# Handing out attention pieces in every second step of the first layer's loop, in groups of about four

## The chip, the cores and the metric

The kernel runs on one core of one Trainium2 chip. Times are device microseconds of one execution. The kernel before took 1786.16 us, the median of 3 runs (1785.07 to 1788.48).

## The reference

Attention over pooled keys and values, and two feed-forward layers behind it, all in float32:

```python
# q, k, v: (8 batches, 8 heads, 576 tokens, 64)
k_p = k.reshape(B, H, 72, 8, D).mean(axis=3)      # v_p in the same way
scores = softmax(q @ k_p.T / 8)                   # (576 x 72) for each batch and head
attn = scores @ v_p
x = attn.transpose(0, 2, 1, 3).reshape(4608, 512)
h = x @ w_in;  x1 = (h - tanh(h)) @ w_out         # 512 -> 2048 -> 512
h = x1 @ w2_in;  out = (h * cos(h)) @ w2_out      # the same sizes
```

## The kernel before, in words

**The layers.** The 4608 tokens go through each layer in 9 blocks of 512 (`i` from 0 to 8). A block has 16 steps (`f`), one for each 128 of the 2048 inner columns. A step of the first layer has 12 matmuls of 128x512 for `h` (`emit_h`, line 553), the elementwise work of `h - tanh(h)` on ScalarE and VectorE (`g1_act`, `g1_rest`, lines 564 to 576), the split of its result into a high and a low part (`g_second`, lines 582 and 583), and 12 matmuls that add an earlier step's part to the four accumulators (`emit_out1`, line 590). Numbers are carried as pairs of high and low parts, hence three matmuls for one product. `h` has two PSUM banks, the accumulators four.

**The attention.** It makes the `x` of the first layer, two blocks ahead of its use, in a ring of 1536 tokens (`xh`, `xl`). It is cut into pieces, and a list `items` holds them in a fixed order (lines 417 to 514). Batches are cut into tiles of up to 128 queries. A tile has `s1` (four transposes of q, line 332, evacuated by ScalarE at 334), `s2` twice (four score matmuls each, line 346; VectorE takes the maxima and subtracts them, lines 349 and 353, then ScalarE takes the exponential), `norm` on VectorE and GpSimd (lines 360 to 364), `s3` in two parts (four transposes at 375, two at 385; evacuated at 382 and 383, and at 391 to 393), and two or three tiles together have four `pv` (up to four matmuls, line 406; evacuated at 409 and 413). `kprep` (line 302) sets up the keys of a batch. All of these write to the two banks of `ps_a` through `att_tile`, in turn: a piece can't start before the piece two before it has been evacuated. Each piece has loads (`look` asks for those of the pieces up to `LOOK` = 4 ahead) and work that follows it (`post`: pooling of keys and values on GpSimd, `norm`, `place_v`). Some pieces are marked `apart`: they need what the piece just before them makes.

**Who gives them out.** At the head of each step of the first layer `slot` pops pieces (line 908). `index_for` says how many must be done by the end of block `i` (36, 55, 19, 30, 35, 35, 35 and 15 in blocks 0 to 7; five of the 55 only load). `slot` spreads them evenly: by the end of step `f` the share (f+1)/16 is due. It stops ahead of a piece that is `apart`, unless it is the first of the slot or the step is the last of the block.

**What sets the order.** Block 0 also converts the first layer's weights (`w1_tick`), blocks 1 to 7 those of the second layer (`w2_conv`). Until block 8 a planner puts each engine's instructions in order: where an engine is free by its modelled times, it takes the first instruction in program order that is ready by them. So an instruction whose inputs or whose buffer aren't ready lets later ones pass. On the chip each engine's order is then fixed. DMAs are issued from SP.

Of the kernel before, what the change touches and what calls it, by code (L numbers as in the profile page):

```python
# [38 lines left out]
def fused_kernel(ctx: ExitStack, tc: tile.TileContext, q, k, v, w1i, w1o, w2i, w2o, out):  # L39
# [8 lines left out]
    NF = DFF // 128  # L48
# [368 lines left out]
    items = []  # L417
# [98 lines left out]
    pos = [0]  # L516
# [14 lines left out]
    def pop():  # L531
        run_later()
        look(pos[0] + 1 + LOOK)
        it = items[pos[0]]
        pos[0] += 1
        fn = it["work"]()
        if fn:
            later.append(fn)
        later.extend(it["post"])
# [158 lines left out]
    block = [-1, 0, 0]  # L698

    def slot(want, i, f):  # L700
        if block[0] != i:
            block[:] = [i, want - pos[0], 0]
        due = -(-block[1] * (f + 1) // NF)
        first = True
        while block[2] < due and (first or f == NF - 1 or not items[pos[0]]["apart"]):
            pop()
            block[2] += 1
            first = False
# [84 lines left out]
    if True:  # L793
# [91 lines left out]
        for i in range(NB):  # L885
# [8 lines left out]
            for f in range(NF):  # L894
# [11 lines left out]
                else:  # L906
                    wi, wo = ring_i.pop(f), ring_o.pop(f)
                slot(want, i, f)
                do_second()
                run_later()  # L910
# [80 lines left out]
```

## Time and profile before

| | |
|---|---|
| median of 3 runs | 1786.16 us (1785.07 to 1788.48) |
| the profiled execution | 1787.28 us, span 1785.5 us |
| TensorE busy | 1737.2 us, 97% of the span |
| VectorE, ScalarE, GpSimd busy | 70%, 65%, 16% |
| mean granted TensorE clock | 0.989 of full speed |
| first layer, first matmul of block 0 to the end of block 8 | 59.20 to 992.24 us of the span |

The span splits in three: 59 us of attention before the first dense matmul, the nine blocks of the first layer with attention beside them, and nine blocks of the second layer, each of 16 like steps. Shares of busy time of TensorE are those of pipelined matmuls with modelled ends, so the distance between two starts says more than a duration.

### The profile page before, as it was taken

What the parts mean: (1) busy time and instruction counts of PE and PEld (TensorE: products, weight loads), DVE (VectorE), ACT (ScalarE), POOL (GpSimd) and SP (SyncE); (2) the same over time, 40 slices, a digit from 0 to 9 for tenths busy, and PEclk for the clock granted to TensorE, in tenths of its full rate; (3) what the DMA queues carried; (4) which work ended last, traced back from release to release, by engine and by line L of the source; (5) the groups of instructions that cost most, each with busy time, mean ns of one, the idle gap of its engine ahead of it and who ended that gap; (6) DMA issues with size and microseconds to landing.
All of it is one profiled execution on the core that took longest, in us unless ns stands there. A gap on an engine that the chain in (4) does not pass through costs nothing.

```text
span 1785.5 us, 22632 instructions
## 1 busy us (share of the span) xinstructions
PE 1737.2 (97%) x7960; PEld 1426.6 (80%) x7960; DVE 1244.2 (70%) x2109; ACT 1158.1 (65%) x2079; POOL 279.2 (16%) x342
## 2 busy tenths in 40 slices
PE   5989999999999999999999999999999999999999
PEld 3666878888888888888888888888888888888887
DVE  8699778778888887776666566565656666566655
ACT  4576767767677776766665666666666666666665
POOL 3764244213424141100000000000000000000000
PEclk8799999999999999999999999999999999999999
DMA  7565655645655554523277401010101010101000
GB/s 234 162 215 192 211 161 182 212 159 185 205 177 184 188 197 142 175 100 109 83 262 254 154 0 48 1 48 1 48 1 47 1 47 1 48 1 48 1 24 24
DMA packets 116402, 202.29 MB, mean 113 GB/s; under 512 B 45376, under 2 KB 61760, under 8 KB 116288
## 3 DMA queue, kind: packets, MB, share of 16 engines
q1 hardware_dynamic: 116288, 200.84, 33.9%
q8 instruction: 63, 1.03, 0.2%
q14 instruction: 51, 0.42, 0.1%
HBM read 156.76 MB, written 44.04 MB: 112 GB/s over the span
## 4 chain that ended last, share of the span: by engine, by line
PE 86%; DVE 5%; DMA 3%; ACT 2%; POOL 2%; issue 1%; SPq 0%; POOLq 0%; DVEq 0%; ACTq 0%
PE h L751 22%; PE acc L779 21%; PE h L553 19%; PE acc L590 18%; PE att L406 2%; PE att L346 2%; DMA kv<-in_k_dram 1%; POOL kv L269 1%; PE att L375 1%; DVE cva L168 1%; DMA raw<-in_moe_w_in_dram 1%; DVE gl L583 1%; DVE w L576 1%; PE att L332 1%; DVE w L575 1%
## 5 line engine op out<-in xcount | busy, mean ns | idle before, releaser
L751 PE MATMUL h<-xh,wi 128*128 128x512 f32 x1008 | 330.8, 389 | 0.0
L779 PE MATMUL acc<-wo,gh 128*128 128x512 f32 x1008 | 310.3, 389 | 0.0
L762 DVE SCALAR_TENSOR_TENSOR r<-kk,h 128x512 f32<-128x512 f32 (+1 forms) x145 | 99.1, 684 | 182.2 <-ACT kk L760 181.8
L751 PEld LDWEIGHTS h<-xh,wi 128*128 128x128 f32 x1008 | 189.3, 188 | 39.4
L779 PEld LDWEIGHTS acc<-wo,gh 128*128 128x128 f32 x1008 | 189.2, 188 | 39.3
L770 ACT ACTIVATE r<-r 128x512 f32<-128x512 f32 (+1 forms) x145 | 91.3, 630 | 195.2 <-DVE r L764 195.2
L553 PE MATMUL h<-xh,wi 128*128 128x512 f32 x576 | 199.8, 407 | 1.2 <-POOL wi L162 0.6
L553 PE MATMUL h<-xh,ri 128*128 128x512 f32 x576 | 196.2, 400 | 0.0
L571 DVE SCALAR_TENSOR_TENSOR w<-u,h 128x512 f32<-128x512 f32 x144 | 98.2, 682 | 140.6 <-ACT th L565 140.5
L751 PE MATMUL h<-xl,wi 128*128 128x512 f32 x504 | 196.1, 389 | 0.0
L779 PE MATMUL acc<-wo,gl 128*128 128x512 f32 x504 | 196.1, 389 | 0.0
L772 DVE TENSOR_TENSOR co<-co,h 128x512 f32<-128x512 f32 (+1 forms) x145 | 99.1, 684 | 117.6 <-ACT co L771 117.6
L590 PE MATMUL acc<-gh,wo 128*128 128x512 f32 x576 | 178.9, 392 | 0.0
L590 PE MATMUL acc<-gh,ro 128*128 128x512 f32 x576 | 177.4, 389 | 0.0
L759 ACT ACTIVATE kk<-h,bias_r 128x512 f32<-128x512 f32 (+1 forms) x145 | 99.6, 687 | 91.6 <-PE h L751 91.6
L564 ACT ACTIVATE u<-h 128x512 f32<-128x512 f32 x144 | 85.6, 594 | 91.6 <-PE h L553 91.1
L582 ACT ACTIVATE gh<-w 128x512 fp32r<-128x512 f32 x144 | 90.9, 631 | 66.3 <-DVE w L576 65.2
L583 DVE TENSOR_TENSOR gl<-w,gh 128x512 fp32r<-128x512 f32 x144 | 109.7, 762 | 28.2 <-ACT gh L582 26.0
L553 PEld LDWEIGHTS h<-xh,wi 128*128 128x128 f32 x576 | 109.7, 191 | 24.4 <-POOL wi L162 1.1
L590 PEld LDWEIGHTS acc<-gh,wo 128*128 128x128 f32 x576 | 109.1, 190 | 22.9
L576 DVE COPY_PREDICATED w<-u,th 128x512 f32<-128x512 uint32 x144 | 113.3, 787 | 19.1 <-ACT u L574 6.1
L590 PEld LDWEIGHTS acc<-gh,ro 128*128 128x128 f32 x576 | 108.1, 188 | 22.5
(165 smaller groups left out, 3530.4 us busy)
## 6 DMA issues: line engine op xcount, KB each, us to landing
ri<-s1i SPq DMA_DIRECT2D x64, 512.0 KB, 3.5
ro<-s1o SPq DMA_DIRECT2D x64, 512.0 KB, 3.4
raw<-in_moe_w_in_dram SPq DMA_DIRECT2D x32, 512.0 KB, 3.9
raw<-in_moe_w_out_dram SPq DMA_DIRECT2D x32, 512.0 KB, 4.0
x1s<-xe SPq DMA_DIRECT2D x36, 256.0 KB, 4.7
xr<-x1s SPq DMA_DIRECT2D x36, 256.0 KB, 3.9
out_dram<-xe SPq DMA_DIRECT2D x36, 256.0 KB, 2.1
kv<-in_k_dram SPq DMA_DIRECT2D x32, 256.0 KB, 3.9
```

The source lines that it names most:

```text
L553: nc.tensor.matmul(out=h[:, off:off + m], lhsT=wi[:, c, wsel, :], rhs=xt[:, r:r + m], start=(n == 0), stop=(n == 3 * KC - 1))
L571: nc.vector.scalar_tensor_tensor(w, u, C2, h, op0=ALU.mult, op1=ALU.mult)
L576: step_end[0] = nc.vector.copy_predicated(w, u.bitcast(U32), th)
L582: nc.scalar.activation(out=gh[:, a:e], in_=w[:, a:e], func=AF.Copy)
L583: nc.vector.tensor_tensor(gl[:, a:e], w[:, a:e], gh[:, a:e].bitcast(F32), op=ALU.subtract)
L590: nc.tensor.matmul(out=acc[d], lhsT=wo[:, wsel, d * 128:(d + 1) * 128], rhs=gt, start=(f == 0 and n == 0), stop=(f == NF - 1 and n == 2))
L751: nc.tensor.matmul(out=h, lhsT=wi[:, c, wsel, :], rhs=xt[:, o:o + BLK], start=(n == 0), stop=(n == 3 * KC - 1))
L759: nc.scalar.activation(out=kk[:, a:e], in_=h[:, a:e], func=AF.Identity, bias=bias_r, scale=INV_2PI)
L762: nc.vector.scalar_tensor_tensor(r[:, a:e], kk[:, a:e], -PI2_HI, h[:, a:e], op0=ALU.mult, op1=ALU.add)
L770: nc.scalar.activation(out=r[:, a:e], in_=r[:, a:e], func=AF.Abs)
L772: nc.vector.tensor_tensor(co[:, a:e], co[:, a:e], h[:, a:e], op=ALU.mult)
L779: nc.tensor.matmul(out=acc[t], lhsT=gt[:, t * 128:(t + 1) * 128], rhs=wo[:, wsel, :], start=(f == 0 and n == 0), stop=(f == NF - 1 and n = ...
```

## The change

In blocks 1 to 7 the odd steps get no pieces, and an even step gets what is due up to the end of the odd step behind it; a piece that is `apart` no longer ends the slot. In block 0 an even step gets the share of both steps too, an `apart` piece still ends the slot, an odd step gets what was left over, and the last two steps take all.

```diff
     def slot(want, i, f):
         if block[0] != i:
             block[:] = [i, want - pos[0], 0]
-        due = -(-block[1] * (f + 1) // NF)
+        due = -(-block[1] * (f + 2 - f % 2) // NF) if f % 2 == 0 or i == 0 else block[2]
         first = True
-        while block[2] < due and (first or f == NF - 1 or not items[pos[0]]["apart"]):
+        while block[2] < due and (first or f >= NF - 2 or i > 0 or not items[pos[0]]["apart"]):
             pop()
             block[2] += 1
             first = False
```

By the code, the pieces that do work in the 16 steps of a block are, before and after:

```
block 0: 3 2 2 2 3 2 2 2 3 1 3 2 3 2 2 2    5 0 4 0 5 0 4 0 4 1 4 0 3 2 4 0
block 1: 1 2 2 4 4 3 4 3 2 5 3 4 3 4 2 4    7 0 2 0 7 0 7 0 7 0 7 0 7 0 6 0
block 2: 2 1 1 1 1 2 1 1 1 1 2 1 1 1 1 1    3 0 2 0 3 0 2 0 2 0 3 0 2 0 2 0
block 3: 2 2 2 2 2 2 2 1 2 2 2 2 2 1 3 1    4 0 4 0 4 0 3 0 4 0 4 0 4 0 3 0
block 4: 3 2 2 2 2 3 2 1 3 2 3 2 2 2 2 2    5 0 4 0 5 0 4 0 4 0 5 0 4 0 4 0
blocks 5 and 6: as block 4
block 7: 1 1 1 1 1 1 1 1 1 1 1 1 1 1 1 0    2 0 2 0 2 0 2 0 2 0 2 0 2 0 1 0
```

## Rows read from the trace of the kernel before

**Rows 1.** The page's chain that ended last, by engine.
```profile
PE 86%; DVE 5%; DMA 3%; ACT 2%; POOL 2%; issue 1%; SPq 0%; POOLq 0%; DVEq 0%; ACTq 0%
```

**Rows 2.** Windows: length, busy time (instructions) by engine, granted clock; blocks 0, 1, 2, 3-6, 7, 8.
```profile
59.20:184.50 125.30, 112.77 (x494) 86.14 (x493) 109.14 (x167) 87.33 (x175) 71.00 (x79) 0.95 0.64 211
184.50:303.34 118.84, 114.26 (x573) 93.78 (x572) 92.06 (x179) 82.80 (x176) 45.94 (x65) 0.99 0.55 176
303.34:399.49 96.15, 96.15 (x457) 79.89 (x456) 71.20 (x123) 66.01 (x119) 21.86 (x25) 1.00 0.55 181
399.49:811.32 411.83, 409.93 (x2025) 341.23 (x2024) 331.73 (x593) 293.58 (x578) 108.64 (x131) 1.00 0.52 172
811.32:905.20 93.88, 93.88 (x437) 77.73 (x436) 62.26 (x105) 58.00 (x102) 2.29 (x2) 1.00 0.33 112
905.20:992.24 87.04, 87.04 (x385) 72.07 (x384) 55.65 (x85) 52.74 (x89) 0.00 (x0) 1.00 0.71 260
```

**Rows 3.** Waits of TensorE in block 0: total us, times, longest.
```profile
PE att L375 <- DVE eb L353: 5.7, 2, 3.8
PE att L406 <- DVE xl L413: 2.3, 1, 2.3
```

**Rows 4.** Waits of TensorE in block 1, the largest group.
```profile
PE att L375 <- DVE eb L353: 3.8, 2, 3.5
```

**Rows 5.** Waits of TensorE in blocks 2 to 7, all groups.
```profile
PE att L346 <- DVE ar L393: 0.9, 1, 0.9
PE att L346 <- ACT qT L334: 0.6, 1, 0.6
PE att L375 <- POOL kv L269: 0.4, 1, 0.4
```

**Rows 6.** Timeline of TensorE (start, length, what): lone pieces in block 2.
```profile
314.88 0.60 PE L375 MATMUL att<-ident,eb 128*128 128x128 f32 x4
315.23 0.48 PE L553 MATMUL h<-xh,wi 128*128 128x512 f32 x1
315.55 0.40 PE L553 MATMUL h<-xl,wi 128*128 128x512 f32 x1
...
320.81 0.38 PE L385 MATMUL att<-ident,eb 128*32 128x128 f32 x2
320.94 0.48 PE L553 MATMUL h<-xh,ri 128*128 128x512 f32 x1
```

**Rows 7.** Timeline of TensorE: the same two pieces in one slot, block 1.
```profile
196.52 0.60 PE L375 MATMUL att<-ident,eb 128*128 128x128 f32 x4
...
197.10 0.48 PE L553 MATMUL h<-xh,wi 128*128 128x512 f32 x1
```

**Rows 8.** Timeline of TensorE: a third piece of a slot, block 5.
```profile
604.01 0.66 PE L346 MATMUL att<-bd,qT 128*96 128x144 f32 x4
604.41 0.49 PE L553 MATMUL h<-xh,wi 128*128 128x512 f32 x1
604.75 0.73 PE L346 MATMUL att<-bd,qT 128*96 128x144 f32 x4
605.23 0.49 PE L553 MATMUL h<-xl,wi 128*128 128x512 f32 x1
605.55 0.62 PE L553 MATMUL h<-xh,wi 128*128 128x512 f32 x2
```

**Rows 9.** Timeline of TensorE: a third value piece, block 1.
```profile
295.62 0.40 PE L553 MATMUL h<-xh,ri 128*128 128x512 f32 x1
296.52 0.39 PE L406 MATMUL att<-ah,vbd 128*128 128x320 f32 x1 [0.51 <-DVE xl L413]
```

**Rows 10.** Timeline of VectorE: two score pieces evacuated, block 4.
```profile
502.27 0.80 DVE L349 TENSOR_REDUCE mx<-att 96x4 f32<-96x288 f32 x2
503.00 0.80 DVE L353 TENSOR_TENSOR eb<-att,mx 96x288 f32<-96x288 f32 x2
```

**Rows 11.** Window around the long wait of block 1 (columns as in rows 2).
```profile
226.60:238.80 12.20, 8.69 (x41) 7.01 (x40) 10.23 (x19) 9.10 (x18) 5.00 (x6) 0.86 0.49 164
```

## The prediction, made before the changed kernel was run

> **What bounds the kernel now.** I read the page first: the chain that ended last is 86% TensorE, 5% VectorE, 3% DMA [rows 1]. The change touches only the attention pieces, and those run beside blocks 0 to 7 of the first layer, so the second view is a table of windows over that layer (a window runs from the first matmul of a block's first step to that of the next block; blocks 3 to 6 stand together) [rows 2]. Block 8 holds no attention: 87.04 us for 16 steps, so a step of 12 + 12 dense matmuls costs 5.44 us, 0.227 us a matmul. What a block has above 87.04 us is what its attention costs. Counting the code's list, blocks 0 to 7 get 36, 50, 19, 30, 35, 35, 35 and 15 pieces that do work (block 1 gets five more that only load):
>
> - blocks 2 to 7: 9.11 us in block 2, 411.83 - 4 x 87.04 = 63.67 us in blocks 3 to 6, 6.84 us in block 7: 79.6 us over 169 pieces, 0.471 us a piece. The reader should see that it doesn't hang on density: 0.48 in block 2 and 0.46 in block 7 at about one piece a step, 0.47 in blocks 3 to 6 at two.
> - block 1: 31.80 us over 50 pieces at three or more a step, 0.64.
> - block 0: 38.26 us over 36 pieces, 1.06. Weights are converted here too: VectorE is busy 109.1 of 125.3 us, and TensorE's clock was granted at 0.95 of full, against 1.00 from block 2 on.
>
> The third view, who waited for whom on TensorE, says how much of this is waiting: 8.0 us in the two largest groups of block 0 [rows 3], 3.8 us in the largest of block 1 [rows 4], and only 1.9 us in all of blocks 2 to 7 [rows 5]. So in blocks 2 to 7 the attention is nearly at the cost of its own matmuls: there is little left that another grouping could win there, and much that it could lose.
>
> **The change part by part.** No work is added or removed: the same 260 pieces run in the same order, each with its matmuls, evacuations and loads. What moves is when they are handed out.
>
> *Fewer borders between attention and dense matmuls.* One could hope that four pieces together save borders. A lone piece of four transposes takes 0.35 us to the first dense matmul, and that one 0.32 to the next instead of 0.227, so 0.09 for the border; a lone piece of two transposes takes 0.13 us to the dense matmul, 0.22 with such a border [rows 6]. The same two pieces in one slot take 0.58 us [rows 7]: with one border 0.67 us, against 0.35 + 0.09 + 0.22 = 0.66 apart. The border saved comes back in that it is only the last transpose before dense work that the next matmul overlaps. I take 0; the bounds are 0 and a gain of 0.09 us for each of some 40 borders less in blocks 2 to 7, 3.6 us.
>
> *Pieces that find both spare PSUM banks taken.* All pieces of these blocks write to two buffers (`ps_a`), so from the third piece of a slot on each needs the evacuation of the piece two before it. From the code: third and later pieces of a slot number 5, 19, 0, 1, 4, 4, 4, 0 in blocks 0 to 7 now, and 17, 34, 3, 14, 19, 19, 19, 0 after: 61 more in blocks 2 to 7, 15 more in block 1, 12 more in block 0. What such a piece does now can be seen. The planner doesn't let TensorE stand: it slips the piece in between the dense matmuls of the same step, where it reckons the bank to be free. In [rows 8] the third piece of a slot comes behind one dense matmul: that one takes 0.34 us to the piece instead of 0.227 (+0.11), the piece takes 0.48 us to the next dense matmul, and that one 0.32 (+0.09): 0.68 us. The like piece ahead of it takes 0.40 us, 0.49 with a border. So a piece that is slipped in costs 0.19 us more than one at a border, without a wait worth the name. A less lucky one is the third of four value pieces in [rows 9]: TensorE stood at it for VectorE's evacuation, 0.90 us instead of 0.23, +0.67. VectorE shows why: the two score pieces of one slot are evacuated together, 0.80 + 0.80 us one behind the other, and the first bank is given back only by the second of those pairs [rows 10]. With four or five pieces in a slot that queue is twice as long, while what the planner reckoned with is not what the chip does. What is queued behind a waiting piece is everything on TensorE, since its matmuls run in order.
>
> Bounds for one more third-or-later piece: 0 (the planner finds a place where the bank has been free for long) and 0.67 us. The value in between I take from density. Block 1 is the one block that already runs at the new density (three to four a step). Without its one long wait of 3.5 us [rows 4] and the slow clock around it (granted 0.86 over 12.2 us, so about 1.7 us lost) [rows 11] its pieces cost (31.80 - 5.2) / 50 = 0.53 us, 0.06 us above the 0.471 of blocks 2 to 7. For the 135 pieces of blocks 3 to 6 that is 8.2 us, or 0.135 us for each of the 61 third-or-later pieces: between 0 and the 0.19 of [rows 8], as when some get through free. Block 1 itself: 15 x 0.135 = 2.0 us; its first slot now also holds one tile's whole chain (transposes, scores, softmax, transposes, values), which stood in four steps. I put that into the same price.
>
> *Empty odd steps.* They run at 5.44 us and let ScalarE and VectorE catch up; in blocks 3 to 6 VectorE is busy 331.7 of 411.8 us [rows 2], so nothing was owed there. Worth 0.
>
> *Block 0.* Pieces come up to half a step earlier, five and four together, against a VectorE that has 13% left. The waits there could shrink or grow; the bounds are -4 us (half of the 8.0 us) and +4. I take 0.
>
> *Loads.* Each pop asks for the loads of four pieces ahead. With four in two steps instead of two in each the lead is the same two steps; in block 1, with seven in a slot, it is shorter for the last three. Loads are issued where their buffers come free, so I take 0 and leave up to 2 us in the range.
>
> Sum: 8.2 + 2.0 = +10.2 us. The profiled execution took 1787.28 us (span 1785.5), 1.1 above the median of 1786.16: 1797.5 on its own scale, **1796.4 us** against the median.
>
> The Trainium skill, Perfetto Trace Analysis, section Optimization Strategy, holds that the same gap repeating on the engine that ought to be saturated can mean too little PSUM for the next tile to be allocated. By that rule every third and fourth piece would show a gap as in [rows 9]. The trace so far agrees only in part: [rows 9] shows such a gap, [rows 8] none, and the sum by the rule is the last rival's.
>
> **Rivals.** (1) *Faster: the long waits of blocks 0 and 1 go.* Place: the 3.5 us at the third piece of a slot of block 1 with its slow clock, 5.2 us, and half of block 0's 8.0 us [rows 3]. Both are accidents of order: TensorE waits there for a VectorE instruction that releases a bank [rows 3, 4]. Another order moves them, and an empty step behind each full one lets VectorE drain before the next. If the inserted pieces then cost nothing: 1786.2 - 5.2 - 4 = 1777 us. It decides if the planner reckons VectorE's evacuations right, so that pieces slip in free as most do now. For it: blocks 2 to 7 wait only 1.9 us with 13 such pieces. Against: those waits came in the two blocks that have most pieces in a slot. (2) *No difference:* the planner, which orders by what is ready and not by slots, spreads the pieces over both steps again, and TensorE's order is nearly the old one: 1786 us, give or take 3. For it: pieces are already found in the middle of dense runs; against: an order by readiness puts them into the first free place, not at the next border. (3) *Every third-or-later piece waits as in [rows 9]*: 76 x 0.67 = 51 us, 1837 us. Against: most of those seen now don't.
>
> **How the numbers follow.** Forecast 0.53, rival 1 0.27, rival 2 0.15, rival 3 0.05. The forecast's own range is 1790 to 1808 (0.06 to 0.28 us for each of the 76). Since cases of both signs hold much of the chance, the whole range takes in rival 1 and stops short of rival 3: 1777 to 1815. Within 0.2% (1782.6 to 1789.7 us, about what can be told from no change): 0.16, rival 2 and an edge of its neighbours; slower 0.57; faster 0.27.
>
> **What would show it right or wrong.** Block 8 and the second layer must stay at 87.04 us a block. Right: blocks 3 to 6 each 1.5 to 3 us longer, their even steps carrying pieces between dense `h` matmuls with gaps before them released by the evacuations of lines 334, 353, 383, 393 or 413, and odd steps at 5.44 us. The empty odd steps failing to show would be rival 2; blocks 3 to 6 unchanged with blocks 0 and 1 shorter would be rival 1. The prediction is wrong at its root if a piece that is slipped in costs no more than one at a border.

## The result, and the profile after

The changed kernel took 1809.43 us, the median of 4 runs (1806.94 to 1811.89), beside 1786.01 for the kernel before on the same chip: ratio 1.0129, 95% interval 1.0107 to 1.0151. It is 23.4 us slower; forecast were 10.2. The profiled execution took 1811.87 us (span 1810.1): of the four, two took 1807.0 us at a mean granted clock of 0.988 and 0.989, and two, this one among them, 1811.9 us at 0.984 and 0.986.

The page's chain that ended last, by engine, of the kernel after (before: [rows 1]):

```profile
PE 83%; DVE 6%; POOL 4%; ACT 3%; DMA 2%; issue 2%; SPq 0%; POOLq 0%; DVEq 0%; ACTq 0%
```

TensorE's share of the chain fell from 86 to 83%. GpSimd's, ScalarE's and VectorE's rose by 2, 1 and 1 points, though their work is the same.

Windows of the kernel after over blocks 0, 1, 2, 3 to 6, 7 and 8 (columns as in [rows 2]: length, then busy time and instructions of TensorE, its weight loads, VectorE, ScalarE and GpSimd, then granted clock, DMA share, GB/s):

```profile
58.95:192.79 133.84, 114.95 (x495) 87.93 (x493) 108.54 (x167) 89.06 (x176) 72.49 (x79) 0.92 0.59 196
192.79:312.80 120.01, 115.65 (x573) 93.55 (x572) 92.75 (x175) 81.85 (x174) 49.92 (x69) 0.99 0.56 181
312.80:411.93 99.13, 96.47 (x457) 79.89 (x456) 76.48 (x127) 67.09 (x121) 20.22 (x21) 1.00 0.52 170
411.93:836.33 424.40, 416.34 (x2030) 343.14 (x2028) 332.66 (x594) 294.80 (x579) 109.17 (x131) 0.99 0.51 167
836.33:929.61 93.28, 93.22 (x434) 77.31 (x432) 61.92 (x104) 57.25 (x102) 2.30 (x2) 1.00 0.33 113
929.61:1016.65 87.04, 87.04 (x386) 72.07 (x384) 55.66 (x85) 52.77 (x89) 0.00 (x0) 1.00 0.72 261
```

Against [rows 2] that is +8.5 us in block 0, +1.2 in block 1, +3.0 in block 2, +12.6 in blocks 3 to 6, -0.6 in block 7, 0 in block 8: 24.6 us, the whole difference of the two spans. Block 8 and the blocks of the second layer stay at 87.04 us from start to start. The busy times of the other engines hardly move (VectorE 332.7 against 331.7 us in blocks 3 to 6). TensorE has the same matmuls, but its row rises by 6.4 us there (409.9 to 416.3), the other 6.2 of the 12.6 us are idle time. Part of the 6.4 is the clock, as the four blocks show one by one (before: 101.67, 103.25, 103.69 and 103.22 us, all at 1.00):

```profile
411.93:519.02 107.09, 103.81 (x496) 84.90 (x495) 82.20 (x142) 72.12 (x141) 34.55 (x42) 0.98 0.55 177
519.02:626.79 107.77, 105.30 (x515) 86.85 (x513) 86.05 (x156) 75.83 (x152) 35.27 (x44) 0.98 0.56 182
626.79:732.24 105.45, 103.68 (x514) 85.61 (x513) 85.03 (x151) 75.31 (x148) 28.43 (x36) 1.00 0.54 176
732.24:836.33 104.09, 103.55 (x515) 85.78 (x513) 79.37 (x148) 71.54 (x141) 10.92 (x9) 1.00 0.39 131
```

In blocks 3 and 4 the granted clock fell to half (1.2 GHz instead of 2.4) for 3.4 us each, within 1.2 us of the end of TensorE's waits of 1.8 and 2.4 us, and TensorE was busy all through; the second of these stretches, same columns:

```profile
589.84:593.26 3.42, 3.42 (x12) 2.73 (x11) 3.33 (x9) 2.44 (x7) 1.11 (x2) 0.50 0.03 8
```

At half the clock that is about 1.7 us lost each, 3.4 us in all, an estimate. Blocks 4 to 6 hand out the same numbers of pieces in the same steps, yet they grew by 4.5, 1.8 and 0.9 us: the cost is in a few places, not spread over the pieces. In block 6, which pools no keys and values, GpSimd is busy 10.9 us against 35.3 in block 4.

Waits of TensorE in block 0 of the kernel after, the three largest groups (total us, times, longest; before: [rows 3]):

```profile
PE att L385 <- ACT ah L380: 8.9, 2, 7.9
PE att L406 <- DVE xl L413: 3.5, 1, 3.5
PE att L375 <- POOL eb L364: 2.7, 1, 2.7
```

The same view of blocks 2 to 7, all groups shown (before: [rows 5], 1.9 us in all):

```profile
PE att L375 <- DVE eb L353: 2.4, 1, 2.4
PE att L346 <- ACT qT L334: 1.8, 2, 1.6
PE att L346 <- DVE xl L413: 1.8, 1, 1.8
PE att L385 <- ACT bd L318: 1.7, 1, 1.7
PE att L385 <- DVE al L383: 1.0, 1, 1.0
PE att L332 <- DVE al L383: 0.8, 2, 0.5
PE att L406 <- DVE ar L393: 0.5, 1, 0.5
PE att L406 <- DVE xl L413: 0.4, 1, 0.4
```

All eight groups end at an instruction that empties an attention bank: 10.4 us. (The 0.5 us behind line 393 can also be a value piece's wait for its own input.) What delays an evacuation is seen by following one back. The timeline of the kernel after around the wait of 1.7 us in block 5 (start, length, engine, line, what; in brackets the idle time before it and its releaser), lines of GpSimd, ScalarE, VectorE and TensorE picked out:

```profile
648.97 1.51 POOL L269 TENSOR_TENSOR kv<-kv 128x256 f32<-128x256 f32 x2 [2.56 <-DMA kv<-in_k_dram]
...
652.08 1.72 POOL L162 TENSOR_TENSOR w2st<-cva,w2st 128x512 fp32r<-128x512 f32 x1
...
653.83 0.67 ACT L157 ACTIVATE cva<-raw 128x512 f32<-128x512 f32 x1 [1.68 <-POOL w2st L162]
654.41 0.44 ACT L313 ACTIVATE bd<-att 64x72 f32<-64x72 f32 x2
654.76 0.19 ACT L318 ACTIVATE bd<-att 64x48 f32<-64x48 f32 x1
...
652.77 1.63 DVE L576 COPY_PREDICATED w<-u,th 128x512 f32<-128x512 uint32 x1
...
652.46 0.55 PE L375 MATMUL att<-ident,eb 96*128 96x96 f32 x4
652.80 0.47 PE L553 MATMUL h<-xh,wi 128*128 128x512 f32 x1
655.00 0.34 PE L385 MATMUL att<-ident,eb 96*32 96x96 f32 x2 [1.73 <-ACT bd L318]
```

Read it from the top. GpSimd stood 2.56 us for a transfer of keys and then worked without a pause, so that its part of the weight conversion (L162) ended at 653.80. ScalarE's next instruction in order, the conversion's first (L157), needs the buffer that this frees, and stood 1.68 us. Behind it in ScalarE's order were the copies that empty the bank of the group's first piece (`kprep`, transposed at 652.05). The group's third piece, L385, writes to that bank, and so TensorE stood 1.73 us with dense matmuls behind it. Before the change a third piece was rare (13 in blocks 2 to 7, 74 after), and holds of ScalarE passed unseen. They were no shorter: ScalarE's idle time ahead of lines 157 and 272 in blocks 2 to 7, two lines before and two after (count, busy us and mean ns, idle us before them and who ended it):

```profile
L157 ACT ACTIVATE cva<-raw 128x512 f32<-128x512 f32 x25 | 16.9, 674 | 11.4 <-DMA raw<-in_moe_w_out_dram 5.8 <-DMA raw<-in_moe_w_in_dram 3.9 <-POOL w2st L162 1.8
L272 ACT ACTIVATE kp<-kp 128x320 f32<-128x320 f32 x4 | 1.9, 472 | 6.8 <-POOL kp L270 6.8
```
```profile
L157 ACT ACTIVATE cva<-raw 128x512 f32<-128x512 f32 x25 | 16.8, 670 | 7.6 <-DMA raw<-in_moe_w_out_dram 3.6 <-DMA raw<-in_moe_w_in_dram 2.2 <-POOL w2st L162 1.7
L272 ACT ACTIVATE kp<-kp 128x320 f32<-128x320 f32 x3 | 1.4, 471 | 4.9 <-POOL kp L270 4.9
```

That is 18.2 us of holds beside 1.9 us of TensorE's waits before, and 12.5 beside 10.4 after. The wait of 2.4 us in block 4 goes the same way round by VectorE: ScalarE stood for GpSimd's sum of keys, VectorE then for ScalarE's tanh (line 565), and its evacuation at line 353 came behind the step's own work. In block 3 the hold is only 0.5 of the 1.8 us.

```profile
582.74 0.47 ACT L272 ACTIVATE kp<-kp 128x320 f32<-128x320 f32 x1 [2.28 <-POOL kp L270]
584.22 0.69 DVE L571 SCALAR_TENSOR_TENSOR w<-u,h 128x512 f32<-128x512 f32 x1 [3.03 <-ACT th L565]
```

Block 0's long wait is of the same kind. The timeline there, same columns:

```profile
99.95 0.60 PE L375 MATMUL att<-ident,eb 128*128 128x128 f32 x4
...
108.72 0.31 POOL L270 TENSOR_TENSOR kp<-kv 64x64 f32<-64x64 f32 x1
...
109.07 0.47 ACT L272 ACTIVATE kp<-kp 128x320 f32<-128x320 f32 x1 [5.36 <-POOL kp L270]
109.45 0.70 ACT L574 ACTIVATE u<-u,bias_m 128x512 f32<-128x512 f32 x1
110.06 0.65 ACT L157 ACTIVATE cva<-raw 128x512 f32<-128x512 f32 x1
110.61 0.58 ACT L380 ACTIVATE ah<-att 128x512 f32<-128x512 f32 x1
...
111.25 0.61 PE L385 MATMUL att<-ident,eb 128*32 128x128 f32 x2 [7.90 <-ACT ah L380]
```

ScalarE stood 5.36 us for GpSimd's last sum of keys; the evacuation at line 380 was three instructions behind. This evacuation empties the bank of the transposes at 99.95, the piece directly ahead of L385: here the piece waited for the one before it, so the two banks don't always come strictly in turn, and the piece waited for isn't always the one two before.

### The profile page after: what moved, and what is told of

It reads as the page before. It is cut to its first block, busy times and chain, and to the rows that moved or that the text cites. A ratio compares the mean times of both kernels' runs of the same rounds, so it can differ in the third digit from the quotient of the medians.

```text
span 1810.1 us, 22625 instructions
## 1 busy us (share of the span) xinstructions
PE 1745.1 (96%) x7960; PEld 1428.0 (79%) x7960; DVE 1250.1 (69%) x2109; ACT 1160.5 (64%) x2079; POOL 283.6 (16%) x342
## 4 chain that ended last, share of the span: by engine, by line
PE 83%; DVE 6%; POOL 4%; ACT 3%; DMA 2%; issue 2%; SPq 0%; POOLq 0%; DVEq 0%; ACTq 0%
PE h L751 21%; PE acc L779 21%; PE h L553 18%; PE acc L590 16%; PE att L406 2%; PE att L346 2%; POOL kv L269 2%; DMA kv<-in_k_dram 2%; DVE w L575 1%; PE att L332 1%; DVE w L571 1%; DVE cva L168 1%; PE att L375 1%; DVE w L576 1%; ACT u L564 1%
## 5 line engine op out<-in xcount | busy, mean ns | idle before, releaser
L751 PE MATMUL h<-xh,wi 128*128 128x512 f32 x1008 | 330.7, 389 | 0.0
L553 PE MATMUL h<-xh,wi 128*128 128x512 f32 x576 | 207.1, 415 | 0.4 <-POOL wi L162 0.4
L571 DVE SCALAR_TENSOR_TENSOR w<-u,h 128x512 f32<-128x512 f32 x144 | 98.5, 684 | 133.9 <-ACT th L565 133.5
L553 PE MATMUL h<-xh,ri 128*128 128x512 f32 x576 | 189.6, 390 | 0.0
L590 PE MATMUL acc<-gh,wo 128*128 128x512 f32 x576 | 183.7, 397 | 0.0
L583 DVE TENSOR_TENSOR gl<-w,gh 128x512 fp32r<-128x512 f32 x144 | 113.6, 789 | 43.7 <-ACT gh L582 39.6
L269 POOL TENSOR_TENSOR kv<-kv 128x256 f32<-128x256 f32 (+7 forms) x154 | 116.0, 757 | 81.5 <-DMA kv<-in_v_dram 38.4
L576 DVE COPY_PREDICATED w<-u,th 128x512 f32<-128x512 uint32 x144 | 114.6, 796 | 19.7 <-ACT u L574 6.3
```

What stands on the lines that cost most here:

```text
L269: nc.gpsimd.tensor_tensor(t[:n, :w], t[:n, :w], t[:n, w:2 * w], op=ALU.add)
L553: nc.tensor.matmul(out=h[:, off:off + m], lhsT=wi[:, c, wsel, :], rhs=xt[:, r:r + m], start=(n == 0), stop=(n == 3 * KC - 1))
L571: nc.vector.scalar_tensor_tensor(w, u, C2, h, op0=ALU.mult, op1=ALU.mult)
L576: step_end[0] = nc.vector.copy_predicated(w, u.bitcast(U32), th)
L583: nc.vector.tensor_tensor(gl[:, a:e], w[:, a:e], gh[:, a:e].bitcast(F32), op=ALU.subtract)
L590: nc.tensor.matmul(out=acc[d], lhsT=wo[:, wsel, d * 128:(d + 1) * 128], rhs=gt, start=(f == 0 and n == 0), stop=(f == NF - 1 and n == 2))
```

## The experiments

Three theories run through the expectations. **B**: a group's third and later pieces wait for one of two banks, so their number sets the price. **H**: holds in ScalarE's order (it waits for GpSimd or a transfer, and evacuations stand behind) are what the banks pass on. **A**: pieces that are `apart` no longer end a slot, and wait for their own forerunner. (P, that each slipped-in piece costs about the same, and G, that the grouping itself costs, are told in the expectations that use them.) Block lengths are those of each run's one profile, and differ between profiles with the same rule there: block 0 under the old rule took 123.5 to 126.5 us, block 1 116.5 to 118.9. Medians of before beside them lie between 1784.2 and 1786.8 us.

**Where: block 0, and blocks 1 to 7.** The new rule only in block 0, then only in the others:

```diff
-        due = -(-block[1] * (f + 1) // NF)
+        due = -(-block[1] * (f + 2 - f % 2) // NF) if i == 0 else -(-block[1] * (f + 1) // NF)
...
-        while block[2] < due and (first or f == NF - 1 or not items[pos[0]]["apart"]):
+        while block[2] < due and (first or f >= NF - 1 - (i == 0) or not items[pos[0]]["apart"]):
```
```diff
-        due = -(-block[1] * (f + 1) // NF)
+        due = -(-block[1] * (f + 1) // NF) if i == 0 else -(-block[1] * (f + 2) // NF) if f % 2 == 0 else block[2]
...
-        while block[2] < due and (first or f == NF - 1 or not items[pos[0]]["apart"]):
+        while block[2] < due and (first or f == NF - 1 or i > 0 or not items[pos[0]]["apart"]):
```

> The new rule in block 0 alone, the old one in blocks 1 to 7. The traces put 8.5 of the 24.5 us into block 0. Theory H (ScalarE is held up in order by a copy of the pooled keys that waits for GpSimd, and with pieces waiting for a bank this reaches TensorE): about 1794 us, since block 0's wait of 7.9 us is of this kind. Theory P (each piece slipped in between dense matmuls costs about the same): 12 of the 88 additional ones are in block 0, so 1786 + 3 = 1789 us. Blocks 1 to 7 within 2 us of before under both.

> The new rule in blocks 1 to 7 alone, block 0 as before. By the traces the rest of the difference, 16 us: about 1802 us under theory H, with waits at other places than in the changed kernel, since GpSimd's and the DMAs' work stands elsewhere against the steps; 1786 + 20 = 1806 us under theory P (76 of 88 additional pieces). If block 0's order is what disturbs blocks 2 to 7 too, within 3 us of before.

Measured: 1792.57 (ratio 1.004, 1.0024 to 1.0055) and 1803.09 us (1.0102, 1.0078 to 1.0127), against 1785.41. So 7.2 and 17.7 us: together 24.9, about the 23.4 of the change. Both lie nearer to H's numbers than to P's. Block 0 alone went from 125.3 to 133.5 us, with the same wait of 7.9 us.

**Odd steps instead of even ones, and `apart` ending the slot as before.**

```diff
-        due = -(-block[1] * (f + 1) // NF)
+        due = -(-block[1] * (f + 1) // NF) if i == 0 or f % 2 else block[2]
...
-        while block[2] < due and (first or f == NF - 1 or not items[pos[0]]["apart"]):
+        while block[2] < due and (first or f == NF - 1 or i > 0 or not items[pos[0]]["apart"]):
```
```diff
-        due = -(-block[1] * (f + 1) // NF)
+        due = -(-block[1] * (f + 2 - f % 2) // NF) if i > 0 else -(-block[1] * (f + 1) // NF)
```

> As e2, with the odd steps giving out instead of the even ones (what is due up to their own end). The same number of third-or-later pieces (108), everything half a step to a step later against the loads and the conversions. Theory B: 1803 us within 5, with long waits at other places. If e2's loss is an accident of where its pieces fall, it could be anywhere between 1786 and 1815 us.

> As e2, but a piece that is apart ends the slot again in blocks 1 to 7, and what is left goes to the odd step. Third-or-later pieces 97 instead of 108. Theory B: 1786 + 17 x 65 / 76 = about 1800 us. Theory A (pieces that stand right behind what they need are what costs): 1790 us or less.

Measured: 1807.97 (1.0129, 1.0112 to 1.0146) and 1803.06 us (1.0105, 1.0089 to 1.0122). Blocks 2 to 7 grew by 18.3 and 13.0 us, 0.30 and 0.23 us for each of the 61 and 57 more third-or-later pieces. Which steps are empty matters little (4.9 us between odd and even), and theory A, which asked 1790 us or less, falls.

**Fewer third pieces with the same empty steps.** Half of an even step's group stands ahead of its `h` matmuls, half ahead of its output matmuls (29 third-or-later pieces in blocks 1 to 7 instead of 108):

```diff
...
+        if i > 0 and f % 2 == 0 and part == 1:
+            due = (block[2] + due + 1) // 2
...
                 gq.append((i, f, wo, w))
+                if i > 0:
+                    slot(want, i, f, 2)
+                    run_later()
```

> As e2 (blocks 1 to 7 grouped, block 0 as before, 1803 us), but an even step gives half of its pieces at its head and the other half between its h matmuls and its output matmuls; odd steps stay empty. Third-or-later pieces of one handing out fall from 108 to 29 in blocks 1 to 7 (32 before the change). Theory B (two banks: a third piece waits for the evacuation of the first, and the waits are TensorE's): 1788 us within 4. Theory G (it is the grouping itself: full steps overload VectorE and ScalarE, empty ones leave them idle): 1803 us within 4.

Measured: 1797.21 us (1.0071, 1.0056 to 1.0086), between B's number and G's. Blocks 2 to 7 came back to within 3.2 us of before, from 15.2 with the group whole. Block 1 didn't: 125.95 us, with one wait of 5.4 us, though it had 20 third-or-later pieces there against 19 before: their number is not all that counts. The same for block 0, in the kernel that has the new rule only there:

> Only block 0 is grouped in even steps, but half of each group stands ahead of the hidden matmuls and half ahead of the output matmuls: 4 third-or-later pieces in block 0 where the run with the new rule in block 0 has 17. Theory B: most of that run's 7 us comes back, about 1787.5 (1785 to 1790). Rival (block 0 pays for the order in which its pieces come, with GpSimd's sum late, not for their number in a group): about 1792 (1790 to 1796), with a wait of 6 us or more at a value piece's or probability's transposition.

Measured: 1785.07 us (0.9995, 0.9986 to 1.0005), and block 0 at 126.7 us. All of block 0's loss came back.

**The other way: nine to fourteen pieces in every fourth step** of blocks 1 to 7 (`f + 4`, `f % 4`), and **one piece at a time**, given out twice in every step of the kernel before:

> Blocks 1 to 7 give out in every fourth step, 9 to 14 pieces together: 163 third-or-later pieces there against 32 of the kernel before and about 108 when given out in every second step. If each costs the same 0.245 us: 1786 + 131 x 0.245 = 1818 (1811 to 1826). If the price lies in a group's first waits (ScalarE's holds meet a group once, however long it is): no more than every second step costs, 1798 to 1806.

> The other way round: block 0 as before, in blocks 1 to 7 pieces are given out twice in every step, ahead of the h matmuls and ahead of the output matmuls, so that one handing out holds about one piece; third-or-later pieces fall from 32 to 1. Theory B: faster than before by what waits and slipped-in pieces cost there now, 5.3 us in block 1, 1.9 us in blocks 2 to 7 and 31 x 0.1 us: 1776 to 1782 us. Theory G: 1786 us within 2. If borders cost after all (some 110 more of them at 0.09 us): 1790 us or more.

Measured: 1814.13 (1.0161, 1.0145 to 1.0177) and 1789.91 us (1.0026, 1.0015 to 1.0037). Every fourth step: 27.3 us for 131 more third-or-later pieces, 0.21 each, so in the sum the price goes with their number, somewhat below the forecast line. It doesn't in each block: block 6, with 23 more, grew by 0.7 us, block 4, with as many, by 8.4. The pieces one at a time win nothing: B's gain at 19 such pieces in block 1 and 13 in blocks 2 to 7 didn't come. The run is 4.5 us slower, about what the third expectation had, that borders cost after all; by the code it has 78 more handings-out in blocks 1 to 7, not the 110 reckoned there. What made the 4.5 us was not traced.

**Theory H, one hold.** The second copy of the summed keys, for which ScalarE waits (line 272), is made by GpSimd itself, in the kernel after and in the one before:

```diff
             nc.gpsimd.tensor_tensor(o, t[:n, :D], t[:n, D:2 * D], op=ALU.add)
+            if which == "k":
+                nc.gpsimd.tensor_tensor(kp[:n, c, D:2 * D], t[:n, :D], t[:n, D:2 * D], op=ALU.add)
-        if which == "k" and c == NKC - 1:
+        if which == "k" and c == NKC - 1 and b == 0:
```

> The changed kernel, with the second copy of the pooled keys made by GpSimd (its last addition is done twice, 30 instructions more) instead of by one ScalarE copy that waits for GpSimd; batches 1 to 7. Theory H: the waits of TensorE behind that copy go (7.9 us in block 0; 1.7, 1.8 and 2.4 us in blocks 2 to 4, each with its slow clock), 1809 - 15 = 1794 us or less. Theory P: 1809 us within 4, since as many pieces are slipped in. Theory A (pieces that stand right behind what they need, because apart no longer ends a slot): 1809 us within 4 as well.

> The kernel before, with the same replacement of the copy of the pooled keys. Theory H: the wait of 3.5 us in block 1 and its slow clock go, 1781 us, and the gain is smaller than in the changed kernel (5 against 15 us), since here most hold-ups of ScalarE end before a piece needs the bank. Theories P and A: 1786 us within 2.

Measured: 1809.03 (1.0136, 1.0102 to 1.017) and 1787.93 us (1.0016, 1.0007 to 1.0026). Nothing came back. In block 0 the longest wait fell from 7.9 to 3.5 us, but its granted clock fell too, from 0.92 to 0.88, and the block took 136.2 us against 133.8. Taken as this one hold, H falls; GpSimd also had 30 instructions more, and what each of these did wasn't parted. (Of the waits that the expectation names, those of blocks 0, 3 and 4 had a slow clock beside them, that of block 2 had none: it ran at 1.00.)

**Two holds taken away.** With that edit, ScalarE's first conversion reads the first raw piece every time:

```diff
-            w2_raw[n] = raw_load(src_of(w2i, w2o, *w2_pieces[n]))
+            raw = raw_load(src_of(w2i, w2o, *w2_pieces[n]))
+            if n < 1:
+                still.append(raw)
+            w2_raw[n] = still[0]
```

> Blocks 1 to 7 grouped as in the changed kernel, block 0 by the old rule; GpSimd makes the second copy of the summed keys itself in batches 1 to 7, and ScalarE's first weight conversion reads the first raw piece every time, so that it waits for no transfer (all second-layer weights are then made of the first piece). Theory H (ScalarE's instructions held up in order, for GpSimd's sum and for the transfers, are what the two score banks pass on to TensorE): with both holds gone blocks 2 to 7 come within 4 us of the kernel before and the time is about 1790 (1786 to 1794). Theory B (a third piece of a group waits for a bank whatever ScalarE does): the grouped rule still costs 13 to 18 us, about 1802 (1798 to 1807).

> The kernel before with the same two holds of ScalarE taken away, the reference for the grouped run (here too all second-layer weights are made of the first piece). Both theories: 1783 to 1788, since the kernel before has only 1.9 us of waits for buffers in blocks 2 to 7 to lose; theory H would also take part of block 1's 3.5 us wait.

Measured: 1812.93 (1.0156, 1.0139 to 1.0173) and 1803.1 us (1.0098, 1.0083 to 1.0113). The reference was a miss: 16 us slower, so the pair decides nothing between B and H. ScalarE's instructions at the conversion's first line, from 310 to 930 us, in the ungrouped reference (two lines lower there; in the kernel before this stretch has the first of the lines at 157 above):

```profile
L159 ACT ACTIVATE cva<-raw 128x512 f32<-128x512 f32 x25 | 16.6, 664 | 47.2 <-POOL w2st L164 47.2
```

The hold for transfers (9.7 of 11.4 us) gave way to one of 47.2 us for GpSimd. It fits H that with so much hold of ScalarE even groups of two lose, but it doesn't show it: the first edit is in this run too (2.5 us by itself), and transfers moved, by the code because raw pieces no longer waited for a reader. In block 1 the DMA share was 0.76, as the window 185 to 305 us shows, against 0.55 in [rows 2]. Whether this made GpSimd late was not tested.

```profile
185.00:305.00 120.00, 114.15 (x573) 92.92 (x572) 95.92 (x180) 83.36 (x178) 50.67 (x72) 1.00 0.76 243
```

**The conversion left out**, ungrouped and grouped:

```diff
-        nc.sync.dma_start(out=(s2o if s else s2i)[f], in_=rows(w2_st.pop(n)))
+        nc.sync.dma_start(out=(s2o if s else s2i)[f], in_=rows(w2_st[0]))
...
+    def w2_few():
+        yield from converter(w2_pieces[:1], w2_raw, w2_dest, lambda n: None, w2_fin, lambda n: True)
+        for n in range(1, len(w2_pieces)):
+            for _ in range(STEPS - 1):
+                yield True
+            w2_fin(n)
+            yield True
...
```

> The kernel before without the conversion of the second layer's weights in blocks 1 to 7: one piece is loaded and converted, and its result is stored for all 32 (so the second layer computes with one piece's weights). The reference for the grouped run. Both theories: near the kernel before, 1780 to 1787, as that has 1.9 us of waits for banks in blocks 2 to 7 and about 5 us in block 1.

> The same, but blocks 1 to 7 grouped in even steps (block 0 by the old rule). If the waits come from sharing VectorE, ScalarE and GpSimd with the conversion: the grouped rule costs 0 to 6 us over its reference, blocks 2 to 7 within 5 us of it. If two banks are too few for a group whatever else runs: still 12 to 18 us over its reference, as with the conversion (17.7 us). In between, the conversion's part of the price is what is missing from 17.7.

Measured: 1781.69 (0.9982, 0.9972 to 0.9991) and 1787.44 us (1.0022, 1.001 to 1.0033): grouping costs 5.8 us, not 17.7. Windows over blocks 1 and 2 to 7, of the ungrouped kernel and of the grouped one:

```profile
182.05:296.33 114.28, 112.88 (x573) 92.63 (x572) 88.44 (x171) 78.21 (x167) 41.20 (x59) 1.00 0.75 249
296.33:897.38 601.05, 599.32 (x2913) 498.92 (x2912) 430.68 (x766) 391.40 (x746) 97.31 (x132) 1.00 0.39 125
```
```profile
183.01:300.99 117.98, 113.72 (x573) 92.47 (x572) 88.76 (x170) 77.51 (x167) 43.48 (x67) 1.00 0.71 234
300.99:904.31 603.32, 602.08 (x2913) 496.75 (x2912) 434.36 (x768) 390.32 (x746) 89.54 (x125) 1.00 0.40 126
```

Blocks 2 to 7 grew by 2.3 us with the same 61 more third-or-later pieces: 0.04 us each. Block 1 grew by 3.7 us, no less than with the conversion (2.8). All waits of TensorE in blocks 2 to 7 that the view lists for the grouped kernel:

```profile
PE att L346 <- ACT qT L334: 0.6, 1, 0.6
PE att L375 <- POOL kv L269: 0.2, 1, 0.2
PE att L346 <- DVE xl L413: 0.2, 1, 0.2
```

So in blocks 2 to 7 two banks serve groups of four and five if the engines that empty them have time. B alone falls with this: there the price needs both the number and the conversion, whose loads of raw weights went with it.

**The conversion without its holds**: its instructions stay, its last one goes from GpSimd to VectorE, and there are no raw transfers after the first.

```diff
...
+    def converter(pieces, raws, dest, loaded, done, allowed, low=nc.gpsimd):
...
-                nc.gpsimd.tensor_tensor(dlo, pa, dhi.bitcast(F32), op=ALU.subtract)
+                low.tensor_tensor(dlo, pa, dhi.bitcast(F32), op=ALU.subtract)
...
-            w2_raw[n] = raw_load(src_of(w2i, w2o, *w2_pieces[n]))
+            if n == 0:
+                still.append(raw_load(src_of(w2i, w2o, *w2_pieces[n])))
+            w2_raw[n] = still[0]
```

> The kernel before, with the conversion kept but without its holds: no transfer of raw second-layer weights after the first (all pieces are made of it), and the conversion's last instruction on VectorE instead of GpSimd, so that ScalarE's first waits for neither. VectorE gets some 0.8 us more for each of the 32 pieces. The reference for the grouped run: 1780 to 1790.

> The same with blocks 1 to 7 grouped in even steps. If the holds in ScalarE's order make the price: 4 to 9 us over its reference, like the pair without the conversion (5.8). If the time that the conversion takes on VectorE and ScalarE makes it: 13 to 20 us over its reference, since VectorE has more to do than before.

Measured: 1783.27 (0.9996, 0.9986 to 1.0005) and 1796.12 us (1.0068, 1.0052 to 1.0085): grouping costs 12.9 us, between the two expectations and near the lower end of the second. The windows over blocks 2 to 7, ungrouped and grouped:

```profile
298.99:899.89 600.89, 600.05 (x2913) 498.97 (x2912) 484.83 (x848) 418.94 (x798) 99.88 (x131) 1.00 0.44 142
```
```profile
301.48:912.38 610.90, 603.51 (x2913) 497.86 (x2912) 478.44 (x850) 419.04 (x800) 93.22 (x126) 1.00 0.43 140
```

And ScalarE's lines 157 and 272 in the grouped one, blocks 1 to 7: the conversion's hold is down to 1.3 us, but that for the summed keys, which is not the conversion's, was left in (10.0 us; 4.1 in the ungrouped one).

```profile
L157 ACT ACTIVATE cva<-raw 128x512 f32<-128x512 f32 x30 | 20.1, 670 | 1.3 <-DVE w2st L162 1.2
L272 ACT ACTIVATE kp<-kp 128x320 f32<-128x320 f32 x5 | 2.4, 471 | 10.0 <-POOL kp L270 10.0
```

The three pairs make a series for blocks 2 to 7: grouping costs 2.3 us without the conversion, 10.0 with its instructions but not these holds, 15.2 with all (617.0 against 601.9 us). By subtraction, of the 15.2 about 2.3 are there without the conversion, about 8 come with its instructions on VectorE and ScalarE, and about 5 with its holds and what went with them (the raw transfers, GpSimd's part, and one stretch of 3.4 us at half the clock that only the run with all has). The middle share is an upper one: VectorE had an additional instruction there, and the hold for the summed keys had grown. Each number is from one profile of a run, and how it splits further stays open. No run beat the kernel before with all of its work done: the nearest, the split block 0, is level with it.

## Why the prediction was wrong

**The direction and the place were right.** What is lost are mostly waits of TensorE at third-or-later pieces, released by evacuations of the kind that was named, and the clock behind them. Block 8 stayed at 87.04 us. But blocks 3 to 6 were to grow by 1.5 to 3 us each, and grew by 5.4, 4.5, 1.8 and 0.9.

**The failed step: "0.135 us for each of the 61 third-or-later pieces".** Blocks 2 to 7 grew by 14.9 us, 0.245 each, not 8.2. The 0.135 came from block 1's density after its 3.5 us wait and slow clock [rows 4, 11] had been taken off as an accident. That was the mistake: such waits are the price. With them left in, block 1's 0.64 less 0.471 us gives 0.165 x 135 = 22 us, so the measured 14.9 lies between the two readings. The sum held only what a slipped-in piece costs without a wait. TensorE's listed waits went from 1.9 to 10.4 us, 8.5 us more, and the half clock behind two of them took about 3.4 (an estimate): these 11.9 us are the missing term, and of just the two kinds that had been taken off in block 1. The 3.0 us that remain are 0.05 a piece, inside the 0 to 0.19 of [rows 8]. And the price isn't a constant of two banks: it is 0.04 us without the conversion and 0.06 in block 6 with it (0.9 us for 15 more pieces), so VectorE's mean share of busy time (331.7 of 411.8 us), from which I argued that nothing was owed, hid the point. What counts, where a long wait was followed back, is how late the evacuation comes in an engine's order.

**The second failed step: block 0 at 0, bounds -4 to +4.** It cost 8.5 us, 7.2 to 8.2 when changed alone. It has 12 more third-or-later pieces, and is the block where VectorE (87% busy) and GpSimd (57%) are fullest [rows 2]. TensorE's idle time there rose from 12.5 to 18.9 us (length less busy time), and the clock fell from 0.95 to 0.92. By the step's own reasoning it should have carried the highest price, not none.

**Fewer borders, 0 (bound a gain of 0.09 us each).** Block 7 has no third pieces and 15 slots with pieces before, 8 after. It became 0.60 us shorter: 0.086 for each of 7 borders. The bound was the better value; blocks 2 to 6 have some 40 fewer, so their gross price is about 3 us above the net one, an estimate.

**Block 1, +2.0.** Measured +1.2, and +2.8 with block 0 left alone: right as far as it can be told, since the block differs by 2.4 us between profiles with the old rule, and with luck, since its price per piece was that of the failed step. The waits stand at other places than before (the largest is 2.4 us at line 346). **Empty odd steps at 5.44 us**: in block 7, where one piece is slipped in, the even steps' stretch between first `h` matmuls took 5.49 to 5.57 us in seven of the eight. In blocks 3 to 6 the odd steps' stretches took 6.0 to 6.6 us, not 5.44, since I misread what such a stretch would hold: the first two pieces of an even slot stand at the end of the odd step's, the rest between the even step's matmuls. **Loads, 0.** No wait of TensorE for a transfer is listed in blocks 0 to 7, but the chain in block 5 begins with one of GpSimd's.

**The rivals.** (1) fell: another order didn't remove the long waits of blocks 0 and 1; 7.9 us came for 3.8, and 2.4 for 3.5. (2) fell: the order changed. (3) asked 0.67 us for every such piece; most still find a free bank (ten waits listed for 74 such pieces in blocks 2 to 7). The Trainium skill, Perfetto Trace Analysis, section Optimization Strategy, has the rule that goes with it: a repeating gap can mean too little PSUM. The traces agree that the gaps are at bank reuse, and add that with the same two banks they all but went from blocks 2 to 7 (1.0 us) when the emptying engines had less to do.

## What to carry to other kernels

Here, with two buffers, groups of more than two pieces made TensorE wait for the evacuating engines' order, not for their average load. Price such a group in the block where these engines are held up most, and count a long wait seen there, with the slow clock behind it, as part of the price. Before grouping work, follow one evacuation back through its engine's order, and see who that engine waits for: in block 5 a transfer held GpSimd, GpSimd held ScalarE, and ScalarE held TensorE.

## What the runs showed of the hardware

VectorE's instructions with both inputs in SBUF are sometimes stretched while GpSimd works. In the trace of the kernel after, blocks 0 to 7, `L575` took at most 0.77 us in the 95 instances with GpSimd at work for less than 30% of it, and 0.95 us in the mean, up to 1.81, in the other 33; the `L576` in the timeline above took 1.63 us beside GpSimd's `L162`, against 0.75 in the mean of those without. The evacuations at lines 349 and 353, with one input in PSUM, stayed at 0.45 us in both cases. The Trainium skill, SBUF — State Buffer, section Who interferes with whom, has the rule: a VectorE instruction with two SBUF inputs contends with a GpSimd instruction that reads SBUF. These numbers agree. How much of the grouping's price runs through this was not measured.
